# Half of a projection's weights by another queue, two convolutions moved between engines, and a new order of work

## The chip, the core and the metric

The program runs on one NeuronCore of a Trainium2 chip. The core has four compute engines with an instruction queue each, which they work through in order: TensorE (PE; its weight loads are listed as PEld), VectorE (DVE), ScalarE (ACT) and GpSimd (POOL). SyncE (SP) computes nothing here; it issues DMAs. Sixteen DMA engines move data between HBM and the on-chip memory SBUF. Matmuls write to PSUM, eight banks of 512 fp32 columns, and VectorE or ScalarE read the results out of it. Engines wait for one another through semaphores. The metric is the device time of one execution in microseconds; a profiled execution shows when each instruction ran.

## What is computed

Eight batches of an attention without softmax (8 heads, 576 positions, 64 per head), normed per head, followed by a gated feed-forward block with a convolution over three positions:

```
kv  = einsum('bhsd,bhse->bhde', k, v)
out = einsum('bhsd,bhde->bhse', q, kv)
out = out / sqrt(mean(out*out, -1) + 1e-6) * g_norm
x   = out, heads side by side                       # 8 x 576 x 512
h   = max(x @ w_in, 0)                              # 8 x 576 x 1024
c   = conv_w[0]*h[s-1] + conv_w[1]*h[s] + conv_w[2]*h[s+1]
y   = (h * sigmoid(c)) @ w_out                      # 8 x 576 x 512
```

All inputs and the output are fp32 in HBM; the kernel works in bf16 with fp32 sums.

## The kernel before

The kernel is a set of small operations, each a Python function of two to four letters, and a long string ORDER (lines 59 to 135) that names them one by one. The loop at line 779 issues them in that order, and lines 786 to 794 forbid any reordering within an engine. A token such as `hk.0.3.1.0@0` is the operation, its arguments, and after the @ the slots of the buffer rings or PSUM banks that it takes. So ORDER fixes, for each engine on its own, the sequence of work; where an operand isn't ready, the engine stands with all that is behind it. The arguments are mostly b (batch), u (half of the head pairs), s (half of the positions), f (one of 8 blocks of 128 channels of d_ff), j (a pair of such blocks), and for the output p (pair of batches) and m (one of 9 blocks of 128 rows).

What the operations do, by engine:

- Loads. `pre` (247) issues batch 0 in fp32, by the plain queues of SyncE and ScalarE as the table HEAD says (233): q and k by SyncE, v by ScalarE. `cad` and `caa` (389, 392) cast these to bf16 on VectorE and ScalarE. All later batches come by GpSimd's queue, whose DMAs cast on the way: `Lq`, `Lk`, `Lv` (350 to 356); so do `Li` (359, w_in) and `Lo` (364, w_out). `gt` (375) is a tiny GpSimd copy that waits for one of the fp32 tiles and so holds back what GpSimd issues behind it.
- TensorE. `fi` (283) multiplies zeros by zeros, n times 512 columns; it is filler that keeps the array running. `ct` transposes the convolution weights. `qt` (425) transposes q, `kv` (395) makes k-transposed v, `ot` (454) the attention's output, `on` and `oq` (524, 531) sum its squares over each head with a matrix of ones, in whole or in quarters of the array. `hk` (652) is two of the four matmuls of x @ w_in for one f and one half s; `hs` and `hm` are the same for later batches. `cv` (701) is the convolution of one f by six matmuls with an identity and two diagonal matrices, which `dg` (310) prepares on VectorE. `om` (727) is half of y's sum for a row block, `oh` (753) a last row block by column halves.
- VectorE and ScalarE. `qa`/`qd` and `kva`/`kvd` copy q transposed and kv from PSUM (a on ScalarE, d on VectorE). `sq`, `nl` (506, 541): squares and reciprocal square roots on ScalarE; `mo` (555) multiplies the norm in and writes x on VectorE. `rp`, `rh`, `re`: the relu on ScalarE. The convolution of a pair j without TensorE is `ta` for each f, `aa` and `ab` (678 to 692) on VectorE, then `sg` (695) on ScalarE, the sigmoid; with TensorE it is `cv` and `sc` (713, the sigmoid out of PSUM). `mg` (720) multiplies by h. `nl` and the sigmoids need different function tables, and ScalarE loads a table at each change (227).
- Output. `ea` on ScalarE or `ed` on VectorE copy a row block to a slot of the ring "row", `st` stores it by SyncE; `eh`/`dh` and `sh` do it for a column half.

`pl`, `ps`, `pn`, `pg` and `pc` are VectorE's preparations of constants (selection matrices, convolution weights).

In the old order batch 0's blocks 0 to 3 (j = 0 and 1) are convolved on TensorE (`cv.0.2 cv.0.3 cv.0.1 cv.0.0`), all others on VectorE. The first half of w_in is `Li.0.4`, the first cast load that GpSimd issues, after `gt.k.1.0`.

## Time and profile before

| | |
|---|---|
| time, median of 3 runs | 177.79 us (177.78 to 178.52) |
| profiled execution, its span | 175.6 us |
| TensorE busy | 96% of the span |
| VectorE and ScalarE busy | 85% each |
| GpSimd busy | 13% |
| read from HBM, written | 32.52 MB, 9.44 MB |
| cast loads (q0), their packets' time | 14.50 MB, 49.2% of 16 engines' span |
| plain queues (q1) | 13.11 MB, 26.2% |

A row of the profile has a line of the kernel, an engine, an operation, the names out<-in, the tile's partitions x elements with its type, and a count. In the view in order of time the first two numbers are start and duration in us, and a bracket tells how long the engine stood idle before it and what released it. In the view by groups the numbers behind the bar are total busy us and mean ns of one. In the view of stretches each row has from:to, length, then busy us and count for PE, PEld, DVE, ACT and POOL, then the granted share of the TensorE clock, the DMA engines' load and GB/s. The page's rows of digits cut the span in 40 slices of 4.39 us; each digit is the busy tenth. Matmuls overlap in their pipeline, so their single durations are longer than the steps from one to the next.

### The profile page before, as it was taken

What the parts mean: (1) busy time and instruction counts of PE and PEld (TensorE: products, weight loads), DVE (VectorE), ACT (ScalarE), POOL (GpSimd) and SP (SyncE); (2) the same over time, 40 slices, a digit from 0 to 9 for tenths busy, and PEclk for the clock granted to TensorE, in tenths of its full rate; (3) what the DMA queues carried; (4) which work ended last, traced back from release to release, by engine and by line L of the source; (5) the groups of instructions that cost most, each with busy time, mean ns of one, the idle gap of its engine ahead of it and who ended that gap; (6) DMA issues with size and microseconds to landing.
All of it is one profiled execution on the core that took longest, in us unless ns stands there. A gap on an engine that the chain in (4) does not pass through costs nothing.

```text
span 175.6 us, 5070 instructions
## 1 busy us (share of the span) xinstructions
PE 167.9 (96%) x2097; PEld 100.0 (57%) x2114; DVE 149.5 (85%) x290; ACT 148.9 (85%) x268; POOL 22.2 (13%) x35
## 2 busy tenths in 40 slices
PE   7979999999999999999999999999999999999992
...
GB/s 159 392 323 207 207 207 207 208 208 209 207 241 230 227 207 207 170 182 197 258 181 161 14 134 0 119 123 0 119 63 0 0 0 116 13 239 175 179 304 237
DMA packets 25911, 29.11 MB, mean 166 GB/s; under 512 B 6036, under 2 KB 20384, under 8 KB 25888
## 3 DMA queue, kind: packets, MB, share of 16 engines
q0 software_dynamic: 13296, 14.50, 49.2%
q1 hardware_dynamic: 12048, 13.11, 26.2%
q10 hardware_dynamic: 544, 1.18, 1.7%
...
HBM read 32.52 MB, written 9.44 MB: 239 GB/s over the span
## 4 chain that ended last, share of the span: by engine, by line
PE 76%; DVE 12%; ACT 5%; DMA 3%; issue 3%; ACTq 0%; DVEq 0%
PE banks L732 32%; PE banks L628 14%; PE banks L613 9%; PE banks L658 4%; DMA stg<-in_v_dram 3%; PE banks L460 3%; DVE h L722 2%; PE banks L708 2%; ACT taps L698 2%; PE banks L402 2%; PE banks L593 2%; PE banks L433 1%; PE banks L528 1%; DVE taps L681 1%; PE banks L286 1%
## 5 line engine op out<-in xcount | busy, mean ns | idle before, releaser
L732 PE MATMUL banks<-w_out_sb,h 128*128 128x512 bf16 x267 | 62.8, 379 | 1.2 <-issue 0.6
L698 ACT ACTIVATE taps<-taps,cw 128x576 bf16<-128x576 bf16 (+1 forms) x44 | 40.6, 958 | 5.7 <-DVE taps L692 5.5
L732 PEld LDWEIGHTS <-h 128*128 128x128 bf16 x280 | 26.2, 98 | 30.0 <-issue 1.1
L628 PE MATMUL banks<-x,w_in_sb 128*128 128x288 bf16 (+2 forms) x256 | 34.2, 286 | 0.0
L640 ACT ACTIVATE h<-banks 128x288 bf16<-128x288 f32 (+2 forms) x80 | 29.5, 460 | 0.3 <-PE banks L658 0.2
L628 PEld LDWEIGHTS <-w_in_sb 128*128 128x128 bf16 x256 | 24.4, 98 | 7.8 <-issue 0.8
L722 DVE TENSOR_TENSOR h<-h,taps 128x1152 bf16<-128x1152 bf16 (+1 forms) x24 | 22.8, 952 | 1.2 <-ACT taps L698 1.2
L687 DVE TENSOR_TENSOR taps<-taps 128x1152 bf16<-128x1152 bf16 (+1 forms) x22 | 21.5, 978 | 0.5
L509 ACT ACTIVATE sq<-banks 128x576 bf16<-128x576 f32 (+2 forms) x32 | 20.8, 691 | 1.1 <-PE banks L460 1.1
L692 DVE TENSOR_TENSOR taps<-taps,h 128x1152 bf16<-128x1152 bf16 (+1 forms) x22 | 21.4, 972 | 0.3
L681 DVE TENSOR_SCALAR taps<-h,cw 128x576 bf16<-128x576 bf16 (+1 forms) x44 | 18.7, 424 | 0.6 <-ACT h L665 0.5
L682 DVE TENSOR_SCALAR taps<-h,cw 128x576 bf16<-128x576 bf16 (+1 forms) x44 | 18.4, 418 | 0.0
L738 ACT ACTIVATE row<-banks 128x512 f32<-128x512 f32 x23 | 13.5, 597 | 5.7 <-PE banks L732 4.2
L658 PE MATMUL banks<-x,w_in_sb 128*128 128x288 bf16 (+2 forms) x128 | 17.7, 286 | 0.1
L613 PE MATMUL banks<-x,w_in_sb 128*128 128x288 bf16 x128 | 16.9, 286 | 0.0
L556 DVE SCALAR_TENSOR_TENSOR x<-banks,cw,rs 128x576 bf16<-128x576 f32 (+2 forms) x16 | 13.0, 816 | 3.9 <-ACT rs L545 3.6
L658 PEld LDWEIGHTS <-w_in_sb 128*128 128x128 bf16 x128 | 12.0, 98 | 4.4 <-issue 0.5
L227 ACT ACT_TABLE_LOAD x10 | 12.8, 1283 | 2.0 <-issue 1.8
L613 PEld LDWEIGHTS <-w_in_sb 128*128 128x128 bf16 x128 | 12.3, 98 | 3.7 <-issue 0.2
L443 DVE COPY qT<-banks 128x1152 bf16<-128x1152 bf16 (+2 forms) x13 | 8.8, 681 | 5.7 <-PE banks L433 5.7
L545 ACT ACTIVATE rs<-banks,eps_sb 128x576 f32<-128x576 f32 (+2 forms) x16 | 11.8, 740 | 1.1 <-PE banks L528 1.1
L599 DVE SCALAR_TENSOR_TENSOR x<-o,cw,banks 128x576 bf16<-128x576 f32 (+2 forms) x16 | 12.1, 810 | 0.7 <-PE banks L593 0.5
...
## 6 DMA issues: line engine op xcount, KB each, us to landing
...
q_sb<-in_q_dram POOLq DMA_DIRECT2D x6, 576.0 KB, 17.9
k_sb<-in_k_dram POOLq DMA_DIRECT2D x6, 576.0 KB, 14.5
v_sb<-in_v_dram POOLq DMA_DIRECT2D x6, 576.0 KB, 17.9
...
```

What stands on the lines that cost most here:

```text
L509: nc.scalar.activation(T["sq", b, u, s], T["o", b, u, s], AX.Square)
L613: nc.tensor.matmul(ps[:, s, :HS], w_in_sb[:, t, f * P:(f + 1) * P], T["x", b][:, t, c0:c1], start=(t == 0), stop=(t == NT - 1))
L628: nc.tensor.matmul(ps, w_in_sb[:, t, f * P:(f + 1) * P], T["x", b][:, t, c0:c1], start=(t == 0), stop=(t == NT - 1))
L640: nc.scalar.activation(h, fr, AX.Relu)
L658: nc.tensor.matmul(T[at], w_in_sb[:, t, f * P:(f + 1) * P], T["x", b][:, t, c0:c1], start=(t == 0), stop=(t == NT - 1))
L681: nc.vector.tensor_scalar_mul(tap[:, 0, f % 2, :n, 8:8 + S], h[:, f], cw[:, f:f + 1])
L682: nc.vector.tensor_scalar_mul(tap[:, 1, f % 2, :n, :S], h[:, f], cw[:, 2 * NF + f:2 * NF + f + 1])
L687: nc.vector.tensor_add(tap[:, 1, :, :n, :S], tap[:, 0, :, :n, 7:7 + S], tap[:, 1, :, :n, 1:1 + S])
L692: nc.vector.tensor_add(y, y, span(b, n)[:, 2 * j:2 * j + 2])
L698: nc.scalar.activation(y, y, AX.Sigmoid, scale=cw[:, NF + f:NF + f + 1])
L722: nc.vector.tensor_mul(h, h, tap_of(b, j)[:, 1, :, :n, :S])
L732: nc.tensor.matmul(T["om", p, m], h[:, f, m * P:(m + 1) * P], w_out_sb[:, f, :], start=(f == 0), stop=(f == NF - 1))
```

## The change

Batch 0's loads by SyncE are put in another sequence (k's tiles 2 and 3 ahead of the second q), and behind them SyncE loads the first half of w_in in fp32, in two pieces of 256 columns (512 KB each), into two slots of the ring "x". `wd` casts a piece to bf16 on VectorE (`wa`, on ScalarE, isn't used). `Li.0.4` is gone; GpSimd's loads begin after `gt.q.1.1` and come in another sequence. Batch 0's pair j = 1 (blocks 2 and 3) is convolved on VectorE (`ta`, `aa`, `ab`, `sg`) instead of TensorE, and two `dg` are gone. Two of batch 0's casts, one copy of q and two of kv go from VectorE to ScalarE; two `on` become `oq`. The 12 groups of fillers (37 matmuls) become 7 groups (39): 20 ahead of the first transposes, 8 and 4 ahead of the first kv, 7 more up to the first `hk`, none behind it. The order of the whole string is new on every engine, and so are its slots; the output's evictions are shared out differently, several stores are issued later, and both halves of the last row block use slot 5. The number of sigmoid and norm table changes stays 10.

```diff
-    HEAD = (("sync", "q.0.0 k.0.1 k.1.1 q.1.0 k.2.1 k.3.1 q.0.1 q.1.1"), ("scalar", "v.0.2 v.2.2"))
+    HEAD = (("sync", "q.0.0 k.0.1 k.1.1 k.2.1 k.3.1 q.1.0 q.0.1 q.1.1 w.0.2 w.2.2"), ("scalar", "v.0.2 v.2.2"))
...
+    w_rows = moe_w_in.rearrange("(t p) f -> p t f", p=P)
...
-                if x == "q":
+                if x == "w":
+                    T["stw", t] = ring("x", [P, NT, s * P], FP32, "stw")
+                    queue.dma_start(out=T["stw", t], in_=w_rows[:, :, t * P:(t + s) * P])
+                elif x == "q":
...
+    @op
+    def wd(f0, n):
+        nc.vector.tensor_copy(w_in_sb[:, :, f0 * P:(f0 + n) * P], T["stw", f0])
...
-        if u0 == 0:
+        if ("kvb", b) not in T:
...
-        if s == 0:
+        if ("qT", b, u) not in T:
```

The beginning of ORDER:

```diff
-pre@0,1 af cad.q.0.0@0 cad.v.0.0@0 fi.10.512@0 qt.0.0.0@2 qd.0.0.0@0 gt.k.1.0 Li.0.4 fi.9.512@0 ct@0 Lq.1.0.2@1
-Lk.1.0.2@0 Lv.1.0.2@1 Li.4.4 ps pg fi.4.512@1 cad.k.1.0@1 caa.v.1.0 caa.k.0.0 kv.0.0.1@4 kva.0.0.1@0 ot.0.0.0@6 pc
...
-sq.0.1.1@3 oq.0.0.1@0 nl.0.0.1@2 fi.1.512@4 fi.1.512@4 hk.0.1.0.0@4 hk.0.1.0.1 rp.1.0@0 on.0.1.1@0 nl.0.1.1@3
...
-hk.0.2.1.1 qt.1.0.0@6 kv.1.0.1@4 rp.2.1 cv.0.2@2 sc.0.2@0 cv.0.3@0 qd.1.0.0@2 kvd.1.0.1@1 ot.1.0.1@6 sc.0.3 pl
+pre@0,1,0,1 af pl ps caa.q.0.0@0 caa.v.0.0@0 fi.20.512@0 qt.0.0.0@0 qa.0.0.0@0 pn caa.k.0.0@1 cad.v.1.0 fi.8.512@2
+ct@0 pg caa.k.1.0 pc caa.v.2.0 fi.4.512@1 kv.0.0.1@0 kva.0.0.1@0 cad.k.2.0 fi.2.512@2 ot.0.0.0@0 cad.v.3.0 sq.0.0.0@0
+cad.k.3.0 fi.3.512@2 oq.0.0.0@2 cad.q.1.0 kv.0.1.1@4 nl.0.0.0@0 dg.0 qt.0.1.0@6 kva.0.1.1 qd.0.1.0@1 caa.q.0.1
+mo.0.0.0@2 ot.0.1.0@2 sq.0.1.0@0 gt.q.1.1 fi.1.512@4 qt.0.0.1@4 cad.q.1.1 Lv.1.0.2@1 qa.0.0.1 oq.0.1.0@0 dg.1
+qt.0.1.1@6 Li.4.4 nl.0.1.0@0 ot.0.0.1@4 qd.0.1.1 sq.0.0.1@0 wd.0.2 ot.0.1.1@0 Lq.1.0.2@1 sq.0.1.1@1 mo.0.1.0
+fi.1.512@6 oq.0.0.1@6 Lk.1.0.2@0 nl.0.0.1@1 wd.2.2 oq.0.1.1@2 Lq.1.2.2 nl.0.1.1@0 hk.0.0.0.0@6 mo.0.0.1 hk.0.0.0.1
+Lk.1.2.2 hk.0.3.0.0@7 hk.0.3.0.1 mo.0.1.1 hk.0.2.0.0@2 Lv.1.2.2 rp.3.0@0 hk.0.2.0.1 hk.0.1.1.0@3 rp.0.0 hk.0.2.1.0@4
+rp.2.0 Lk.2.0.4@1 hk.0.2.1.1 hk.0.3.1.0@5 rp.2.1 hk.0.3.1.1 Lq.2.0.4@0 hk.0.1.1.1 ta.0.1.2@1 rp.3.1 hk.0.1.0.0@2
+hk.0.1.0.1 rp.1.1 hk.0.0.1.0@4 ta.0.1.3 Lo.0.8 rp.1.0 hk.0.0.1.1 hk.0.5.1.0@5 aa.0.1.1 cv.0.1@0 ab.0.1.1 Lv.2.0.4@0
+qt.1.0.0@2 sc.0.1@0 hk.0.5.0.0@6 qd.1.0.0@0 hk.0.5.1.1 rp.0.1 hk.0.5.0.1 sg.0.1.3 kv.1.0.1@0 Lq.3.0.4@2 cv.0.0@2
+kvd.1.0.1@0 sg.0.1.2 hk.0.7.0.0@4 rp.5.0 mg.0.1.1 qt.1.1.0@0 sc.0.0 ot.1.0.1@6 hk.0.7.0.1 qd.1.1.0@1 sq.1.0.1@0
+hk.0.4.1.0@2 hk.0.7.1.0@3 mg.0.1.0 hk.0.4.1.1 hk.0.7.1.1 oq.1.0.1@0 nl.1.0.1@0 rp.5.1 ot.1.0.0@0 mo.1.0.1@0 rp.7.0
+sq.1.0.0@0 kv.1.1.1@4 ta.0.1.5@0 rp.7.1 Lv.3.0.4@1 on.1.0.0@6 kvd.1.1.1 rp.4.1 ta.0.1.7@1 hk.0.4.0.0@3 nl.1.0.0@0
...
```

Its end:

```diff
-ed.3.7@4 om.3.5.4.4 ea.3.5@3 st.3.5 om.3.4.4.4 ed.3.4@5 st.3.4 st.3.7 om.3.6.4.4 ea.3.6@0 st.3.6 oh.3.8.1@1 eh.3.8.1@2
-sh.3.8.1 oh.3.8.0@0 eh.3.8.0@1 sh.3.8.0
+om.3.5.4.4 ed.3.7@0 om.3.4.4.4 ed.3.5@2 oh.3.8.1@0 st.3.5 ea.3.4@4 om.3.6.0.4@1 dh.3.8.1@5 sh.3.8.1 om.3.6.4.4 st.3.7
+st.3.2 oh.3.8.0@0 st.2.3 ea.3.6@2 st.3.4 st.3.6 eh.3.8.0@5 sh.3.8.0
```

134 lines of the change are left out of this document (64 added, 70 removed).

## The prediction

> **What bounds the kernel now.** I read the page first, then the busy times of four stretches, then TensorE and ScalarE in order of time at the start, then the groups of instructions for prices.
>
> ```profile
> span 175.6 us, 5070 instructions
> PE 167.9 (96%) x2097; PEld 100.0 (57%) x2114; DVE 149.5 (85%) x290; ACT 148.9 (85%) x268; POOL 22.2 (13%) x35
> ...
> PE   7979999999999999999999999999999999999992
> ...
> GB/s 159 392 323 207 207 207 207 208 208 209 207 241 230 227 207 207 170 182 197 258 181 161 14 134 0 119 123 0 119 63 0 0 0 116 13 239 175 179 304 237
> ```
> ```profile
> 0.00:21.20 21.20, 18.64 (x238) 9.22 (x241) 13.91 (x54) 12.27 (x23) 10.69 (x20) 1.00 1.02 260
> 21.20:30.60 9.40, 9.20 (x212) 6.21 (x213) 5.13 (x19) 9.34 (x17) 2.14 (x4) 1.00 1.22 206
> 30.60:172.20 141.60, 140.09 (x1651) 84.57 (x1662) 130.45 (x218) 126.87 (x229) 9.34 (x13) 1.00 0.72 148
> 172.20:175.60 3.40, 0.00 (x0) 0.00 (x0) 0.00 (x0) 0.38 (x1) 0.00 (x0) 1.00 0.54 194
> ```
>
> TensorE is the bound: from 30.6 to 172.2 us it idles 141.60 - 140.09 = 1.51 us in all, and then 3.4 us remain for the last eviction and store. In the first 21.2 us it idles 2.6 us, and part of its busy time there is fillers. From 21.2 to 30.6 ScalarE is as full (9.34 of 9.40) while VectorE has 4.3 us free. So one question decides: by how much is TensorE earlier or later than today when it reaches the work that both kernels have in common after about 30 us? What it is late there, it can win back only out of those 1.51 us.
>
> ```profile
> 1.20 4.45 PE L286 MATMUL banks<-zero 128*128 128x512 bf16 x10 [1.20 <-DVE zero L265]
> 5.57 0.32 PE L433 MATMUL banks<-ident,q_sb 64*64 64x64 bf16 x16
> 5.83 2.12 PE L286 MATMUL banks<-zero 128*128 128x512 bf16 x9
> 7.87 0.24 PE L291 MATMUL banks<-ident,cw_rows 25*128 25x25 f32 x1
> 8.04 1.04 PE L286 MATMUL banks<-zero 128*128 128x512 bf16 x4
> 9.57 0.47 PE L402 MATMUL banks<-v_sb,k_sb 64*64 64x64 bf16 x34 [0.34 <-DVE k_sb L384]
> 13.25 0.30 PE L460 MATMUL banks<-qT,kvb 64*64 64x256 bf16 x4
> 17.64 3.65 PE L658 MATMUL banks<-x,w_in_sb 128*128 128x256 bf16 x28
> 21.22 0.48 PE L433 MATMUL banks<-ident,q_sb 64*64 64x64 bf16 x36
> 30.59 1.15 PE L658 MATMUL banks<-x,w_in_sb 128*128 128x256 bf16 x8
> ```
> ```profile
> 10.10 0.28 ACT L416 ACTIVATE kvb<-banks 128x128 bf16<-128x128 f32 x1 [2.55 <-PE banks L402]
> 14.70 0.69 ACT L545 ACTIVATE rs<-banks,eps_sb 128x512 f32<-128x512 f32 x1
> 21.82 1.28 ACT L227 ACT_TABLE_LOAD   x1
> 27.60 0.74 ACT L545 ACTIVATE rs<-banks,eps_sb 128x576 f32<-128x576 f32 x1
> 16.87 0.91 POOL L365 DMA_DIRECT2D w_out_sb<-in_moe_w_out_dram  x1 [2.30 <-DMA w_in_sb<-in_moe_w_in_dram]
> ```
>
> Columns are start, duration, engine, line, operation, count. The first ten fillers take 0.43 us each (4.45 for ten), the nine at 5.83 only 0.21 (2.12, less 0.2 of latency): TensorE is slow until about 5.5 us. The POOL row shows that the first half of w_in lands at about 16.8, just before the 28 matmuls of 17.64.
>
> **The change, part by part: the first 23 us.** Prices of groups, the last number the mean in ns:
>
> ```profile
> L384 DVE CAST v_sb<-stg 128x576 bf16<-128x576 f32 x2 | 0.9, 457 | 0.2 <-DMA stg<-in_v_dram 0.2
> ...
> L384 DVE CAST q_sb<-stq 128x512 bf16<-128x512 f32 x1 | 0.4, 427 | 1.9 <-DMA stq<-in_q_dram 1.9
> ...
> L386 ACT ACTIVATE v_sb<-stg 128x576 bf16<-128x576 f32 x2 | 1.4, 680 | 2.5 <-DMA stg<-in_v_dram 2.5
> ...
> L443 DVE COPY qT<-banks 128x512 bf16<-128x512 bf16 x2 | 0.8, 414 | 0.0
> ...
> L556 DVE SCALAR_TENSOR_TENSOR x<-banks,cw,rs 128x512 bf16<-128x512 f32 x2 | 1.5, 741 | 0.0
> L556 DVE SCALAR_TENSOR_TENSOR x<-banks,cw,rs 128x640 bf16<-128x640 f32 x2 | 1.8, 884 | 0.9 <-ACT rs L545 0.9
> ...
> L509 ACT ACTIVATE sq<-banks 128x640 bf16<-128x640 f32 x6 | 4.2, 721 | 0.0
> ...
> L665 ACT ACTIVATE h<-banks 128x256 bf16<-128x256 f32 x8 | 3.5, 455 | 0.4 <-PE banks L658 0.4
> ```
>
> Ahead of the first k-v product the old order has 10 + 9 + 4 = 23 fillers, the new one 20 + 8 + 4 = 32, and TensorE keeps the order. Twenty from 1.20: ten at 0.43 to 5.5, ten at 0.21 to 7.6. Then qt.0.0.0 to 7.9 (before 5.57), eight fillers to 9.6, ct, four more to 10.6; kv.0.0.1 stands at 10.7 to 11.2 instead of 9.57 to 10.04. K tile 1 isn't the limit any more: ScalarE casts it after qa.0.0.0 (7.98 to 8.6) and k tile 0, 0.65 us each, by 9.9. So kva.0.0.1 starts at 11.25 (before 10.10).
>
> [...]
>
> ScalarE then goes sq, nl.0.0.0 (13.0 to 13.7), kva.0.1.1 to 14.0. TensorE's ot.0.1.0 stands at 14.1 (before 13.25). Ahead of its square ScalarE now has caa.q.0.1 (0.70), and ahead of nl.0.1.0 the copy qa.0.0.1 (0.65): nl.0.1.0 moves from 14.70 to 15.95. VectorE: four casts moved behind pg and pc end at 13.1; qd.0.1.0 to 14.1, mo.0.0.0 (0.74), cad.q.1.1, dg.1, qd.0.1.1 (0.41, after its transposes) to 16.5.
>
> Then the two new casts of w_in, 1024 elements each. No row has that size: the slope from 512 to 576 (30 ns for 64) gives 0.67 us, proportion to the 457 ns gives 0.81, and twice that, under load from other traffic, 1.6; I take 0.67 as nearest to the rows' own slope. Arrival: at the 392 GB/s of the second slice the three tensors of 1.18 MB are there by about 11.6 and 1.05 MB of w_in by about 14.5, with competition perhaps 16.5, so the landing hides behind the chain. wd.0.2 runs 16.5 to 17.15, mo.0.1.0 to 17.9, wd.2.2 to 18.55, mo.0.0.1 (0.88) to 19.4, mo.0.1.1 to 20.3. What is queued behind the two casts are the three mo of batch 0, and TensorE waits for them. hk.0.3.0.0 needs wd.2.2 and the bank that nl.0.0.1 frees at 18.7; its 28 matmuls at today's 3.65 us end at 22.45. Before, TensorE was through at 21.22: **+1.25 us**.
>
> **From there to 31 us.** Removed on TensorE: two convolutions of six matmuls (one pair in the chain of waits is 1.59 us) and the three fillers that the old order has after this point (0.64). That alone would more than repay the 1.25. But the convolutions' place is taken by two ordinary sets of taps:
>
> ```profile
> 22.05 1.59 PE banks L708 x12
> ```
> ```profile
> L681 DVE TENSOR_SCALAR taps<-h,cw 128x576 bf16<-128x576 bf16 x28 | 10.4, 373 | 0.6 <-ACT h L665 0.5
> L682 DVE TENSOR_SCALAR taps<-h,cw 128x576 bf16<-128x576 bf16 x28 | 10.2, 364 | 0.0
> ...
> L687 DVE TENSOR_TENSOR taps<-taps 128x1152 bf16<-128x1152 bf16 x14 | 10.6, 759 | 0.3
> ...
> L698 ACT ACTIVATE taps<-taps,cw 128x576 bf16<-128x576 bf16 x28 | 20.7, 777 | 5.6 <-DVE taps L692 5.5
> L715 ACT ACTIVATE taps<-banks,cw 128x576 bf16<-128x576 f32 x4 | 2.8, 746 | 0.0
> ```
>
> VectorE gets 2 x (0.37 + 0.36) + 2 x 0.76 = 3.0 us more, which its 4.3 free us cover; two sigmoids from taps for two from PSUM leave ScalarE the same (0.78 for 0.75). ScalarE is the stage's limit, however. Its last rp ahead of the sigmoid table (rp.1.0; the six matmuls behind hk.0.1.0.1 don't concern it) now ends at 22.5, and the table load goes there from 21.82. From it to nl.1.0.1 the new order has: load 1.28, sc 0.7, rp.0.1 0.42, two sg 1.5, rp.5.0 0.42, sc 0.7, sq 0.65, load 1.28 = 6.95 us, against 27.60 - 21.82 = 5.78. So nl.1.0.1 starts at 29.4 instead of 27.60. And TensorE waits for it: oq.1.0.1 and the next ot.1.0.0 are both written at banks 0 and 1, so ot.1.0.0 stands until nl.1.0.1 has read them (30.1), with everything behind it. Then rp.5.1, rp.7.0, sq.1.0.0, rp.7.1 free the bank of hk.0.4.0.0 at about 32.05. In the old kernel those matmuls stand at 30.59, with ot.1.1.1 (0.3) already done: TensorE is **1.75 us late** with the removed 2.2 us of work already counted. Bounds: 0.5 (clock up early, casts 0.67, ScalarE's pieces at their back-to-back spacing) to 3.0 (late clock, casts 1.6).
>
> **After 31 us** the matmuls are the same ones, so the lateness passes through. The idle 1.51 us can shrink to nothing (-1.5) or grow (+2: VectorE gets evictions 1.0, 1.1 and 1.8 that ScalarE had); I take 0. The later start of the cast loads costs nothing: those 0.5 MB of w_in no longer stand ahead of them.
>
> **The tail.**
>
> ```profile
> 172.27 0.38 ACT L767 ACTIVATE row<-banks 128x256 f32<-128x256 f32 x1 [0.54 <-PE banks L757]
> ```
> ```profile
> L777 SPq DMA_DIRECT2D out_dram<-row x2: 333/350/368, 171.8 to 172.7; - x2
> ...
> DMA to landing us min/median/max: 1.9/2.2/2.5
> ```
>
> Both halves of the last row now use row slot 5, so eh.3.8.0 must wait until sh.3.8.1 has landed: from the end of oh.3.8.1 0.4 (eviction) + 0.35 (issue) + 2.2 = 2.95 us, against 2.6 us of matmuls meanwhile (om.3.6 and oh.3.8.0: eight of 512 columns at the 0.21 of the fillers, eight of 256 at half): +0.3 (0 to +0.8, as five full stores queue between the halves).
>
> **Sum**, against the profiled execution: 1.75 + 0 + 0.3 = +2.05 us on a span of 175.6. The median run is 177.79, 2.19 more than that span; the same surplus gives 177.79 + 2.05 = 179.8.
>
> **Rivals.** *TensorE's own work decides* (faster): nl.1.0.1 comes before TensorE needs banks 0 and 1, so nothing holds it between 22 and 30 us. Then the start costs 1.25, the removed 1.59 + 0.64 count in full, and with a third of the later idle gone it is -1.48, 176.3. It decides if nl.1.0.1 starts before 28.3. For it: TensorE is 96% busy; against it: ScalarE's 9.34 of 9.40 and the shared banks. *The lateness is eaten*: 1.75 late at 31, but nearly all of the 1.51 of idle vanishes: 178.2. For it: VectorE and ScalarE have 11.2 and 14.7 us free after 30.6; against it: most of that is behind 140 us or in other places than TensorE's. *ScalarE and VectorE stay behind*: the backlog starves TensorE again in the later stages, +3 more, 182.8; against it, three evictions leave ScalarE.
>
> **How the numbers follow.** The forecast 0.57 (its own range 178.7 to 181.4), TensorE's work 0.15, eaten 0.13, behind 0.15. About 0.9 us either side of 177.79 can't be told from no change: faster 0.15, same 0.13, slower 0.72. The range 176.5 to 182.6 leaves out about half of the first and the last rival.
>
> **What would show it.** Right: k-v product of batch 0 after 10.5 us; qt.1.0.0 after 22; TensorE idle over 1 us before ot.1.0.0, released by ScalarE's L545; the last eviction released by a store. Wrong: the first product still at 9.6, no TensorE idle from 23 to 32 us, or a later idle under 0.8 us.

## The result, and the profile after

The changed kernel takes 188.92 us (median of 4 runs, 186.48 to 190.62) against 177.81 us for the kernel before on the same chip: a ratio of 1.0575, 95% interval 1.0507 to 1.0643. The forecast was 179.8 us with a range to 182.6, so the sign was right and the size was wrong by 9 us. Executions more than 1.5% above the fastest of their kernel (one of the changed kernel's, one each of e2_row and e12_wpool, two of e9_all, one of them its traced one) are left out of the ratios; by its ratio the changed kernel stands at 188.0 us. The profiled execution spans 187.0 us, 11.4 more than the 175.6 of before.

The page of the changed kernel: span, busy time, TensorE's slices and the granted clock.

```profile
span 187.0 us, 5079 instructions
PE 171.6 (92%) x2108; PEld 100.7 (54%) x2108; DVE 150.8 (81%) x290; ACT 152.6 (82%) x272; POOL 21.4 (11%) x34
...
PE   7988997999899979999579999999999999999980
...
PEclk9999998799999999999988999999999999999998
```

TensorE lost four points of its share. The slices, 4.7 us each, show where: at the 7th and 8th TensorE has a dent and the clock another; at the 11th and 15th TensorE alone; at the 20th to 22nd TensorE and then the clock; and the last slice is empty. From the 23rd to the 38th all is full. So the loss isn't one long wait; it sits in a few places, and TensorE's rows in order of time name them. The changed kernel:

```profile
10.37 0.48 PE L415 MATMUL banks<-v_sb,k_sb 64*64 64x64 bf16 x36
17.99 4.35 PE L671 MATMUL banks<-x,w_in_sb 128*128 128x256 bf16 x34 [0.18 <-ACT rs L558]
29.32 0.32 PE L473 MATMUL banks<-qT,kvb 64*64 64x288 bf16 x4 [0.99 <-ACT rs L558]
30.01 0.48 PE L415 MATMUL banks<-v_sb,k_sb 64*64 64x64 bf16 x36 [0.38 <-ACT h L678]
30.86 0.38 PE L671 MATMUL banks<-x,w_in_sb 128*128 128x256 bf16 x2
44.42 0.78 PE L415 MATMUL banks<-v_sb,k_sb 64*64 64x64 bf16 x72
48.62 0.38 PE L446 MATMUL banks<-ident,q_sb 64*64 64x64 bf16 x23 [0.92 <-issue]
69.70 0.71 PE L415 MATMUL banks<-v_sb,k_sb 64*64 64x64 bf16 x64 [1.16 <-issue]
91.00 0.78 PE L492 MATMUL banks<-v_sb,k_sb 64*64 64x64 bf16 x72 [2.38 <-DMA k_sb<-in_k_dram]
96.13 0.70 PE L606 MATMUL banks<-wparts,spread 32*128 32x288 bf16 x4 [1.24 <-ACT h L653]
105.88 0.79 PE L492 MATMUL banks<-v_sb,k_sb 64*64 64x64 bf16 x72
```

The kernel before, the three products that can be matched with it:

```profile
43.17 0.78 PE L402 MATMUL banks<-v_sb,k_sb 64*64 64x64 bf16 x72
...
84.28 0.78 PE L479 MATMUL banks<-v_sb,k_sb 64*64 64x64 bf16 x72
...
96.55 0.79 PE L479 MATMUL banks<-v_sb,k_sb 64*64 64x64 bf16 x72
```

Stretches of the changed kernel, cut where the granted clock changes (the column behind the five engines is the granted clock, PEclk):

```profile
28.25:31.65 3.40, 2.03 (x52) 1.22 (x50) 2.35 (x6) 3.39 (x9) 0.84 (x2) 1.00 1.21 208
31.66:35.06 3.40, 3.40 (x18) 1.68 (x16) 2.19 (x5) 2.52 (x6) 1.37 (x2) 0.50 1.23 206
...
93.10:96.50 3.40, 2.09 (x20) 1.25 (x17) 2.13 (x3) 1.32 (x4) 0.00 (x0) 1.00 0.58 165
96.52:99.92 3.40, 3.40 (x17) 1.51 (x17) 2.14 (x3) 3.21 (x5) 0.00 (x0) 0.50 1.30 198
```

Matching points of equal work gives the lateness step by step. Where the two orders have not done the same work at a point, the difference is added (the kernel before has `ot.1.1.1`, 0.25 us, done ahead of `hk.0.4.0.0`, and `om.0.2.0.4`, four matmuls of 0.21 us, ahead of `kv.2.0.2`). Of the 34 matmuls in the row at 17.99 the last two are `hk.0.5.1.0`, which the kernel before does later, so the first line of the table counts 32.

| TensorE reaches | before | after | late by | what came in |
|---|---|---|---|---|
| end of batch 0's first 32 `hk` matmuls | 21.2 | 21.9 | 0.7 | the start |
| `hk.0.4.0.0` | 30.6 | 30.9 (+0.25) | 0.5 | two convolutions and three fillers gone, waits of 0.99 and 0.38 |
| `kv.2.0.2` | 43.2 | 44.4 (+0.86) | 2.1 | half clock for 3.4 us: 1.6 |
| `kz.6.0.2` | 84.3 | 91.0 | 6.7 | two stops of 0.92 and 1.16, and 2.38 for batch 6's k |
| `kz.7.0.2` | 96.5 | 105.9 | 9.3 | 1.24 for ScalarE, and half clock: 1.4 |
| last matmul's end | 172.2 | 181.5 | 9.3 | nothing: the last 76 us cost the same |
| end | 175.6 | 187.0 | 11.4 | tail 5.5 instead of 3.4 |

Three of these have their cause in rows of other engines. GpSimd issues a k only when its slot is free. The last two k of the changed kernel, and in a second fence the last two of the kernel before:

```profile
70.74 0.74 POOL L352 DMA_DIRECT2D k_sb<-in_k_dram  x1 [13.20 <-PE banks L415]
...
80.38 0.74 POOL L352 DMA_DIRECT2D k_sb<-in_k_dram  x1 [7.42 <-PE banks L473]
```
```profile
67.96 0.74 POOL L347 DMA_DIRECT2D k_sb<-in_k_dram  x1 [2.52 <-PE banks L402]
...
75.01 0.74 POOL L347 DMA_DIRECT2D k_sb<-in_k_dram  x1 [5.57 <-PE banks L460]
```

Before, the first of each two is batch 6 and the second batch 7. In the new order the first is batch 7 and the second batch 6, which is needed 15 us sooner: its load is issued at 80.38 instead of 67.96, and it lands some 10.6 us later, when `kz.6.0.2` has waited 2.38 us for it.

ScalarE's eviction `ea.0.6` waits for a slot of the ring "row" whose store hasn't landed, and the row of SyncE's queue says why (the line's own view gives 2.0 us as the shortest, 2.4 as the median and 11.6 as the longest time from issue to landing):

```profile
95.18 0.60 ACT L751 ACTIVATE row<-banks 128x512 f32<-128x512 f32 x1 [3.33 <-DMA out_dram<-row]
```
```profile
80.82 2.55 SPq L480 DMA_TRANSPOSE qT<-q_sb  x1
83.47 3.60 SPq L761 DMA_DIRECT2D out_dram<-row  x2
```
```profile
DMA to landing us min/median/max: 2.0/2.4/11.6
```

The store stands right behind a DMA transpose and needs 11.6 us. But the DMA engines are full here (a load of 1.0 to 1.4 in stretches of 5 us from 60 to 95 us), and other stores of this stage are slow too, without a transpose right ahead of all of them: those issued at 67.5 to 86.7 us took 5.3 to 8.9 us, and the kernel before has 6.6 to 7.8 us for three of its own at 80 to 85 us. How much of the 11.6 us is the transpose's own isn't shown by any run. TensorE's 1.24 us before L606 are the end of this: `rh` stands behind `ea.0.6` on ScalarE. And the tail:

```profile
179.41 0.33 SPq L790 DMA_DIRECT2D out_dram<-row  x1
179.80 2.75 SPq L761 DMA_DIRECT2D out_dram<-row  x5
...
181.56 0.38 ACT L780 ACTIVATE row<-banks 128x256 f32<-128x256 f32 x1 [0.28 <-PE banks L770]
182.65 0.40 SPq L790 DMA_DIRECT2D out_dram<-row  x1
```

The last eviction is released by TensorE, not by a store, and is done at 181.9. Its store is issued 0.7 us later, because five full stores that the old order spread out are ahead of it, and it lands 4.3 us after its issue.

### The profile page after: what moved, and what is told of

Its sections match the earlier page's. It is cut to its first block, busy times and chain, and to the rows that moved or that the text cites. A ratio compares the mean times of both kernels' runs of the same rounds, so it can differ in the third digit from the quotient of the medians.

```text
span 187.0 us, 5079 instructions
## 1 busy us (share of the span) xinstructions
PE 171.6 (92%) x2108; PEld 100.7 (54%) x2108; DVE 150.8 (81%) x290; ACT 152.6 (82%) x272; POOL 21.4 (11%) x34
## 3 DMA queue, kind: packets, MB, share of 16 engines
q10 hardware_dynamic: 544, 1.18, 1.6%
## 4 chain that ended last, share of the span: by engine, by line
PE 75%; DVE 7%; DMA 6%; ACT 6%; issue 3%; ACTq 0%
PE banks L745 26%; PE banks L641 13%; PE banks L671 10%; PE banks L626 9%; DMA out_dram<-row 6%; PE banks L291 5%; PE banks L446 2%; PE banks L415 2%; PE banks L473 1%; ACT rs L558 1%; DVE taps L695 1%; PE banks L550 1%; PE banks L541 1%; DVE taps L700 1%; DVE h L735 1%
## 5 line engine op out<-in xcount | busy, mean ns | idle before, releaser
L745 PE MATMUL banks<-w_out_sb,h 128*128 128x512 bf16 x280 | 64.3, 379 | 0.0
L711 ACT ACTIVATE taps<-taps,cw 128x576 bf16<-128x576 bf16 (+1 forms) x46 | 41.4, 951 | 2.5 <-DVE taps L705 2.4
L641 PE MATMUL banks<-x,w_in_sb 128*128 128x288 bf16 (+2 forms) x256 | 34.3, 286 | 0.0
L641 PEld LDWEIGHTS <-w_in_sb 128*128 128x128 bf16 x256 | 24.3, 98 | 8.0 <-issue 0.9
L522 ACT ACTIVATE sq<-banks 128x576 bf16<-128x576 f32 (+2 forms) x32 | 21.1, 694 | 2.2 <-PE banks L473 1.6
L700 DVE TENSOR_TENSOR taps<-taps 128x1152 bf16<-128x1152 bf16 (+1 forms) x23 | 22.1, 966 | 0.4
L705 DVE TENSOR_TENSOR taps<-taps,h 128x1152 bf16<-128x1152 bf16 (+1 forms) x23 | 22.1, 962 | 0.2
L694 DVE TENSOR_SCALAR taps<-h,cw 128x576 bf16<-128x576 bf16 (+1 forms) x46 | 19.3, 420 | 1.7 <-ACT h L678 1.3
L695 DVE TENSOR_SCALAR taps<-h,cw 128x576 bf16<-128x576 bf16 (+1 forms) x46 | 19.7, 429 | 0.0
L671 PE MATMUL banks<-x,w_in_sb 128*128 128x288 bf16 (+2 forms) x128 | 19.3, 300 | 0.2 <-ACT rs L558 0.2
L626 PE MATMUL banks<-x,w_in_sb 128*128 128x288 bf16 x128 | 17.9, 298 | 0.0
L671 PEld LDWEIGHTS <-w_in_sb 128*128 128x128 bf16 x128 | 12.4, 102 | 5.2 <-issue 0.8
L626 PEld LDWEIGHTS <-w_in_sb 128*128 128x128 bf16 x128 | 12.7, 101 | 4.7 <-issue 0.7
L558 ACT ACTIVATE rs<-banks,eps_sb 128x576 f32<-128x576 f32 (+2 forms) x16 | 11.8, 743 | 2.9 <-PE banks L541 1.5
L291 PE MATMUL banks<-zero 128*128 128x512 bf16 x39 | 11.2, 428 | 1.2 <-DVE zero L270 1.2
```

The source lines that it names most:

```text
L291: nc.tensor.matmul(ps[:, :w], zero[:, :P], zero[:, :w], start=True, stop=True)
L522: nc.scalar.activation(T["sq", b, u, s], T["o", b, u, s], AX.Square)
L626: nc.tensor.matmul(ps[:, s, :HS], w_in_sb[:, t, f * P:(f + 1) * P], T["x", b][:, t, c0:c1], start=(t == 0), stop=(t == NT - 1))
L641: nc.tensor.matmul(ps, w_in_sb[:, t, f * P:(f + 1) * P], T["x", b][:, t, c0:c1], start=(t == 0), stop=(t == NT - 1))
L671: nc.tensor.matmul(T[at], w_in_sb[:, t, f * P:(f + 1) * P], T["x", b][:, t, c0:c1], start=(t == 0), stop=(t == NT - 1))
L695: nc.vector.tensor_scalar_mul(tap[:, 1, f % 2, :n, :S], h[:, f], cw[:, 2 * NF + f:2 * NF + f + 1])
```

## The experiments

All stand against runs of the kernel before on the same chip (177.6 or 177.7 us each time). Times below are the ratio times 177.6; the changed kernel is 187.8 on this scale, ratio 1.058 (1.051 to 1.064).

| run | base and edit | us | ratio, 95% interval |
|---|---|---|---|
| e1_k6 | after; k slots of batches 6 and 7 exchanged | 189.6 | 1.068 (1.062 to 1.073) |
| e2_row | after; `ea.0.6` on row slot 3 | 185.2 | 1.043 (1.036 to 1.050) |
| e3_k6_row | both | 183.5 | 1.033 (1.031 to 1.035) |
| e4_fill | after; 16 fillers in the gaps at 28 to 30 us | 186.3 | 1.049 (1.046 to 1.052) |
| e5_shift | after; 16 tiny fillers early, no gap filled | 187.9 | 1.058 (1.052 to 1.064) |
| e6_wsync | before; first half of w_in by SyncE | 184.7 | 1.040 (1.036 to 1.044) |
| e7_cvd | before; two convolutions on VectorE | 179.5 | 1.011 (1.010 to 1.013) |
| e8_tail | e3; late stores behind their evictions | 181.4 | 1.021 (1.018 to 1.025) |
| e9_all | e8; 16 fillers in the gaps | 180.2 | 1.015 (1.013 to 1.017) |
| e10_open | e9; ten of the opening fillers 32 wide | 178.5 | 1.005 (1.004 to 1.006) |
| e11_vec | e8; two evictions on VectorE, `kv.1.1.1` moved | 179.8 | 1.013 (1.011 to 1.014) |
| e12_wpool | e9; w_in by GpSimd again | 179.6 | 1.011 (1.009 to 1.013) |
| e13_open_wpool | e10 and e12 together | 178.9 | 1.008 (1.006 to 1.009) |
| e14_vec | e8; two evictions on VectorE | 179.8 | 1.012 (1.011 to 1.014) |
| e15_best | e8; e10, e12 and e14 together | 179.8 | 1.013 (1.010 to 1.015) |
| e16_open_vec | e8; e10 and e14 together | 179.3 | 1.010 (1.007 to 1.012) |
| e17_pool1 | e13; GpSimd's loads in another sequence, 24 fillers | 179.4 | 1.010 (1.008 to 1.012) |
| e18_pool2 | e17; GpSimd's loads released earlier | 177.7 | 1.000 (0.999 to 1.002) |

**The waits at 91 and 96 us.** Three runs: the k slots exchanged, the row slot changed, and both.

```diff
-Lk.7.0.4@1
+Lk.6.0.4@1
...
-Lk.6.0.4@0
+Lk.7.0.4@0
...
-ea.0.6@2
+ea.0.6@3
```

> The changed kernel, but batch 6's k takes the slot that batch 4's k leaves, and batch 7's k the one that batch 5's leaves (it is the other way round in the change). Theory A, two stops in series: TensorE's wait of 2.9 us for batch 6's k (88 to 91 us) goes, but ScalarE still stands until a store has landed at about 95 us and stops TensorE there, so less than 1.5 us is gained. Rival B, the late k alone makes this stage slow: 2.9 us and the half-rate stretch behind it (1.4) are gained, 4 us or more.

> The changed kernel, but the eviction ea.0.6 takes row slot 3 instead of 2, whose store lands 11.6 us after its issue. Theory A (two stops in series): ScalarE's 3.3 us wait for that landing goes, TensorE's stop at 95 us (1.2 us) goes, the wait for batch 6's k stays: 1 to 2.7 us gained, the latter if the half-rate stretch from 96.8 us goes too. Rival B (the late k alone): 0.5 us or less.

> Both edits of the two kernels before together. Theory A: TensorE's idle of 3.7 us between 88 and 96 us goes and, since the array then never idles there, the half-rate stretch behind it (1.4 us) too: 4.5 to 6 us gained, more than the sum of the two alone. Rival B: as with the k alone, about 4 us. Rival C, the half-rate stretches have nothing to do with the stops: 3.7 us, and the granted clock still falls near 97 us.

The first gained nothing (if anything it lost 1%), the second gained 1.4% and both together 2.3%. TensorE's rows of the three show the two waits as stops in series: with the k there in time, TensorE comes to L606 earlier and waits longer for ScalarE, 2.81 us instead of 1.24. First e1_k6, then e2_row, then e3_k6_row:

```profile
95.19 0.60 PE L606 MATMUL banks<-wparts,spread 32*128 32x288 bf16 x4 [2.81 <-ACT h L653]
```
```profile
88.39 0.78 PE L492 MATMUL banks<-v_sb,k_sb 64*64 64x64 bf16 x72 [1.21 <-DMA k_sb<-in_k_dram]
```
```profile
92.12 0.60 PE L606 MATMUL banks<-wparts,spread 32*128 32x288 bf16 x4 [0.24 <-ACT h L653]
```

In the last one TensorE's clock is at 1.00 through these stages. So the two waits and the clock that they cost are worth 4.3 us (187.8 to 183.5), just under the least that theory A said. Rival B had some 4 us for the late k alone; e1_k6, which gained nothing, rules it out. The last row's wait of 0.24 is what is left of both.

**The stops marked "issue".** In the changed kernel TensorE stops for 0.92 and 1.16 us in the middle of one operation, with all operands there. Counted along the order, the two places are behind its 733rd and its 1116th matmul. The difference is 383, three times 128 but one; with a weight load for each (the page has 2108 of both), 128 matmuls are 256 instructions. The page lists 16 packets on the queue "instruction" with 0.26 MB, 16 KB each; TensorE has 2 x 2108 instructions, 264 for each packet, and one such packet moves in the 2 us around each stop's beginning (46 to 48 and 67 to 69 us). From these numbers I estimated that the stops are borders between two blocks of instructions. No run shows what a stop waits for; "border" below means the place in the count. e4_fill puts 16 matmuls into the gaps at 28 to 30 us, e5_shift the same number, 32 columns wide, at 13.8 us, where they fill nothing.

```diff
-ot.0.1.0@2 sq.0.1.0@0
+ot.0.1.0@2 fj.16.0.32@4 sq.0.1.0@0
...
+    def fj(n, c0, w):
+        ps = bank()
+        for _ in range(n):
+            nc.tensor.matmul(ps[:, c0:c0 + w], zero[:, :P], zero[:, :w], start=True, stop=True)
```

> The changed kernel with 12 and 4 short fillers (192 columns, 0.08 us each) in the two gaps of TensorE around 28.3 to 30 us, written to unused columns of a bank. They fill the idle time and remove no wait. Theory A: the clock then stays at full rate from 31 to 35 us, where it was halved for 3.8 us, and 1.9 us are gained (1.4 to 2.2). Rival C (the clock falls for another reason): nothing gained, or 0.3 lost, and the granted clock at 32 to 36 us stays near 0.6.

> The changed kernel with 16 matmuls of 128x32 on zeros more at about 13.8 us, ahead of all else: some 0.5 us of extra work, no idle time filled. Theory F (the stops of 0.92 and 1.16 us in the middle of L446 and L415 hang on how many instructions TensorE has run before them): both stops leave their places, since every later TensorE instruction now stands 32 places (weight load and matmul) further on; if they find no other burst of short instructions, the time falls by 1 to 2 us from the changed kernel's 188.9, and if they only move to another line it stays within 1 us. Rival T (they hang on the time, on other traffic or on an operand): they stay after 49 and after 8 of their instructions, and the time is the same or 0.5 us longer.

In e5_shift both stops left their places; TensorE's row there:

```profile
69.07 0.25 PE L452 MATMUL banks<-ident,q_sb 64*64 64x64 bf16 x7 [0.29 <-issue]
```

Seven of `qt.4.1.0`'s 36 transposes are left, so this border is behind matmul 1117, within one of the number before, now in another operation. e4_fill stops at the same number for 0.29 us, and for 0.84 us behind matmul 1244, some 128 later. e7_cvd, built on the kernel before with 12 matmuls fewer, has a new stop of 1.00 us inside `kv.4.0.2`, behind matmul 1116. The number decides, not the operation, its operand or the time: theory F holds for the place. For the length, the starts of the matmuls in the traces say how fast the 128 ahead of a border went by, from the first start to the last: 3.0 and 2.8 us at the two stops of the changed kernel; about 4.5 us in e4_fill and e5_shift where they don't stop, and 4.6 where they stop for 0.29; 4.7 us and more in the kernel before, which shows no stop. That looks as if only a fast 128 were followed by a long stop. But in e7_cvd the 128 took 3.9 us ahead of a stop of 1.00, and at e4_fill's stop of 0.84 they took 6 us or more. So theory F holds for the place, and what makes a stop long or short stays open. The time of e5_shift is another matter: 187.9 us is no change, where F expected 1 to 2 us less. Its profiled execution gained 1.8 us on the stops and had a half-clock stretch from 18.8 us, as long as the changed kernel's at 31.7, and `ot.1.0.0` at 32.2 instead of 29.3. The time of e4_fill is 1.6 us better, as theory A said, and its trace has no half-clock stretch at 31 us any more, only one from 89.5 us. But the time mixes the filled gaps and the clock with the moved borders and a wait for batch 6's k that grew to 3.15 us, and prices none of them alone.

**The tail.** e8_tail has e3's two mends, and each late store right behind its own eviction:

```diff
-ed.3.7@0 om.3.4.4.4 ed.3.5@2 oh.3.8.1@0 st.3.5 ea.3.4@4 om.3.6.0.4@1 dh.3.8.1@5 sh.3.8.1 om.3.6.4.4 st.3.7
-st.3.2 oh.3.8.0@0 st.2.3 ea.3.6@2 st.3.4 st.3.6 eh.3.8.0@5 sh.3.8.0
+ed.3.7@0 st.3.7 om.3.4.4.4 ed.3.5@2 oh.3.8.1@0 st.3.5 ea.3.4@4 st.3.4 om.3.6.0.4@1 dh.3.8.1@5
+sh.3.8.1 om.3.6.4.4 oh.3.8.0@0 ea.3.6@2 st.3.6 eh.3.8.0@1 sh.3.8.0
```

> The changed kernel with the k slots of batches 6 and 7 exchanged and ea.0.6 on row slot 3 (as in the run of both, 183.6 us), and now also each late store issued right behind its own eviction and the last half row on a slot of its own. Theory P (the five full stores in front of the last one, 2.75 us at 179.8 us, and the shared slot make the tail 5.5 instead of 3.4 us): the tail falls to 3.4 to 3.9 us and the time to 181.5 to 182.2 us. Rival V (the tail is set by how much is still to be moved at the end): it stays above 4.8 us and the time within 0.5 us of 183.6.

```profile
175.22 0.33 SPq L761 DMA_DIRECT2D out_dram<-row  x1
175.52 0.38 ACT L780 ACTIVATE row<-banks 128x256 f32<-128x256 f32 x1 [0.33 <-PE banks L770]
175.93 0.33 SPq L790 DMA_DIRECT2D out_dram<-row  x1
```

The last store is issued when its eviction is done, 175.9, and the kernel ends at 179.0, 3.6 us after the last matmul: 2.1 us gained, theory P.

**The load of w_in, alone.** e6_wsync is the kernel before with SyncE's fp32 load (`w.0.2 w.2.2` at the end of its head) and two casts on VectorE, nothing else but the place of one `dg`:

```diff
-pre@0,1 af cad.q.0.0@0 cad.v.0.0@0 fi.10.512@0 qt.0.0.0@2 qd.0.0.0@0 gt.k.1.0 Li.0.4 fi.9.512@0
+pre@0,1,1,2 af cad.q.0.0@0 cad.v.0.0@0 fi.10.512@0 qt.0.0.0@2 qd.0.0.0@0 gt.k.1.0 fi.9.512@0
...
-qd.0.1.1 mo.0.1.0 ot.0.0.1@2
+qd.0.1.1 mo.0.1.0 wd.0.2 wd.2.2 ot.0.0.1@2
```

> The kernel before with only the first half of w_in by SyncE's queue in fp32 and two casts of it on VectorE after mo.0.1.0 (0.7 us each in the changed kernel's trace): nothing else moved but the two halves of its issue and one diagonal. Theory S (the load and its casts are the dear part of the start): the three mo of batch 0 and with them hk come 1.0 to 1.5 us later, +0.8 to +1.5 us against the kernel before, 178.4 to 179.2. Rival N (the casts hide behind ScalarE's squares and nl): within 0.5 us of the kernel before. Rival G (POOL's load was the wait ahead of hk): 0.5 to 1 us faster.

It cost 7.1 us, far outside all three. VectorE's casts and TensorE behind them, in e6_wsync:

```profile
16.97 0.69 DVE L370 CAST w_in_sb<-stw 128x1024 bf16<-128x1024 f32 x1 [0.89 <-DMA stw<-in_moe_w_in_dram]
21.13 0.69 DVE L370 CAST w_in_sb<-stw 128x1024 bf16<-128x1024 f32 x1 [3.46 <-DMA stw<-in_moe_w_in_dram]
```
```profile
21.88 2.53 PE L671 MATMUL banks<-x,w_in_sb 128*128 128x256 bf16 x11 [3.28 <-DVE w_in_sb L370]
```

The second piece lands at 21.1 us; in the changed kernel, where its cast starts at 17.5, it waits only 0.2 us. What differs is GpSimd's queue. In e6_wsync it issues its first load at 8.4 us, as before, and eight loads, w_out's 1 MB among them, by 14.8; the DMA engines are full (a load of 1.1 to 1.2 from 8.4 to 21.1 us) and SyncE's fp32 pieces share them. In the changed kernel `gt.q.1.1` holds the first of these loads until 13.2, and w_out's is issued at 21.5. This fits the late landing, but no run has e6's load with the later release, so it isn't shown by itself that the later release is what pays for the fp32 load. As it stands, e6's is the worst single edit of this study. TensorE's pause also cost clock: the stretch from 20.2 to 27.0 us has a PEclk of 0.50.

**Two convolutions on VectorE, alone.** e7_cvd moves blocks 2 and 3 of batch 0 to VectorE in the kernel before (the first line of the cut gathers tokens from several places of the order):

```diff
-dg.3 dg.2 cv.0.2@2 sc.0.2@0 cv.0.3@0 sc.0.3
...
-kvd.1.0.1@1 ot.1.0.1@6
+kvd.1.0.1@1 ta.0.1.2@0 ta.0.1.3 aa.0.1.1 ab.0.1.1 cv.0.1@4 cv.0.0@2 sc.0.1@1 sc.0.0 ot.1.0.1@6
...
-mg.0.1.1 Lo.0.8
+sg.0.1.2 sg.0.1.3 Lo.0.8 mg.0.1.1
```

> The kernel before with only two of batch 0's convolutions (blocks 2 and 3) moved from TensorE to VectorE. Theory S (ScalarE bounds 22 to 31 us): TensorE's 1.6 us of work goes, but nl.1.0.1 comes at the same time, so TensorE waits for it in their place: within 0.5 us of the kernel before. Rival W (TensorE's own work decides): 1.0 to 1.6 us faster. Rival L (VectorE's 3 us more delay qd.1.1.0 and batch 1): 0.5 to 2 us slower.

It is 2.0 us slower. TensorE's rows:

```profile
22.71 0.41 PE L708 MATMUL banks<-h,ident 128*128 128x288 bf16 x2 [0.72 <-DVE kvb L414]
...
29.11 0.48 PE L402 MATMUL banks<-v_sb,k_sb 64*64 64x64 bf16 x36 [0.66 <-ACT rs L545]
...
69.36 0.50 PE L402 MATMUL banks<-v_sb,k_sb 64*64 64x64 bf16 x38 [1.00 <-issue]
```

The first of these waits is for VectorE's copy of kv, which is no later than before. Its row in e7_cvd, then in the kernel before:

```profile
22.38 0.28 DVE L414 CAST kvb<-banks 128x128 bf16<-128x128 f32 x1
```
```profile
22.43 0.28 DVE L414 CAST kvb<-banks 128x128 bf16<-128x128 f32 x1
```

What changed is that `cv.0.1` takes bank 4 of `kv.1.0.1` right behind it, where the old order had the two convolutions in between. The second wait, for ScalarE's nl, hangs on the first: the late `cv.0.1` makes `sc.0.1` late, ScalarE stands 0.61 us for it, and nl.1.0.1 starts at 28.31 instead of 27.60. So these two come of the order that this edit chose, and neither rival L (VectorE's added work) nor theory S is shown by them. The third is the border described above, which 12 fewer matmuls moved there. TensorE's busy time fell by 0.9 us (167.9 to 167.0) and its idle time grew by 3.0, of which the three waits are 2.4. The run doesn't price the removal of the convolutions alone.

**The opening fillers, and w_in again.** e9_all puts the 16 fillers of e4 on top of e8. In e10_open ten of the opening twenty are 32 columns wide, which leaves the number of instructions as it is; e12_wpool gives the first half of w_in back to GpSimd; e13_open_wpool has both.

```diff
-fi.20.512@0 qt.0.0.0@0
+fi.10.512@0 fi.10.32@0 qt.0.0.0@0
```

e12's edit, which e13 has too (`w.0.2 w.2.2` goes from SyncE's head, both `wd` go):

```diff
-pre@0,1,0,1
+pre@0,1
...
-kva.0.0.1@0 cad.k.2.0
+kva.0.0.1@0 gt.k.1.0 Li.0.4 cad.k.2.0
```

> The changed kernel with exchanged k slots, ea.0.6 on slot 3, the late stores behind their own evictions (the run at 181.4 us) and 16 matmuls of 128x192 on zeros at 28 to 30 us, where TensorE waits 1.0 and 0.4 us for ScalarE. Theory F (a stop stands where 256 TensorE instructions, loads and matmuls, go by in less than about 4 us, and the 16 pairs move the border out of the burst): the stops of 0.87 and 1.16 us go, one of 0.3 us appears in qt.4.1.0, 179.6 to 179.9 us. Rival T (the stops hang on time or traffic): they stay, and 181.4 us stays. Rival C (the clock falls when TensorE idles, and this is what the fillers mend): no more to gain, since the profile at 181.4 us shows no halved stretch.

> As the run with all mends and the 16 fillers, but ten of the opening twenty matmuls on zeros are 32 columns wide instead of 512: the number of TensorE's instructions stays, 2 to 4 us of opening work goes. Theory O (the opening fillers are what makes batch 0's products late): qt.0.0.0 comes at 5.6 instead of 7.2 to 8 us, the first product of k and v about 0.5 to 1 us earlier, and the time falls by 0.5 to 1.0 us. Rival N (ScalarE's chain of casts and squares sets the start, and fillers only fill): qt.0.0.0 moves, hk.0.0.0.0 does not, within 0.3 us. Rival K (fewer fillers delay the clock): half rate until 8 us or longer, 0 to 1.5 us slower.

> As the run with all mends and the 16 fillers, but the first half of w_in comes by POOL's queue in bf16 as in the kernel before (issued when k tile 1 of batch 0 is there), and VectorE has no cast of it. Theory S (the two casts of 0.7 us hold the mo of batch 0): hk.0.0.0.0 starts 0.7 to 1.4 us earlier and the time falls by 0.5 to 1.2 us. Rival N (ScalarE's nl and sq hold the mo anyway): within 0.3 us. Rival D (POOL's load slows the fp32 loads of q and v): the start is later by 0.5 us or more.

> Ten narrow opening fillers and the first half of w_in by POOL's queue together, on top of all mends and the 16 fillers at 28 to 30 us. Theory S (with the narrow fillers w_in's landing at 15.9 us and its casts hold VectorE, and TensorE waits 1.5 us for them): without the casts this wait goes and 177.3 to 178.0 us. Rival P (POOL's bf16 half lands no earlier than 16.5 us): the wait stays at hk.0.0.0.0, 178.3 to 178.8 us. Rival D (its load delays batch 0's fp32 loads): 179 us or more.

The 16 pairs brought 181.4 to 180.2 us, where F had 179.6 to 179.9. That the two long stops are gone is seen in e10_open and e12_wpool, which keep the pairs: these stop for 0.39 and 0.36 us at matmul 1117, and e12_wpool for 0.29 at 1244. The 1.2 us also holds the gaps that the pairs fill; the two parts aren't separated. F's 256 instructions in under 4 us were an estimate from the counts and the 3.0, 2.8 and 4.5 us above; e4_fill's stop of 0.84 us, behind 6 us or more, doesn't fit it. The narrow fillers gave 1.7 us more, above theory O's 1.0, and brought the kernel to 0.5% above the one before; with GpSimd's load of w_in the same edit is worth only 0.6 to 0.7 us (e12_wpool to e13_open_wpool). What the fillers delay is one step further on than expected: `ct` stands behind them on TensorE, VectorE's `pg` waits for `ct`, and four casts of k, v and q stand behind `pg`. VectorE's row for that step, in e12_wpool with wide fillers, then in e10_open:

```profile
10.63 0.18 DVE L306 COPY cw<-banks 128x25 f32<-128x25 f32 x1 [2.99 <-PE banks L302]
```
```profile
7.93 0.18 DVE L306 COPY cw<-banks 128x25 f32<-128x25 f32 x1 [0.28 <-PE banks L302]
```

The clock has a part in this difference: it rose at 6.6 us in the first of the two executions and at 3.8 us in the second.

With the start early, the load of w_in became the next limit: in e10_open VectorE waits 1.29 us for the first piece until 15.9 and TensorE 1.50 us for the x behind it. With wide fillers GpSimd's load is 0.7 us better than SyncE's with its casts, in the middle of what theory S gave; with narrow fillers it is 0.5 us worse. There the wait of 1.50 is gone, as S said, but TensorE then waits 0.80 us for w_in's second half at 21.5 us. The time, 178.9 us (178.7 to 179.2), lies between rival P's range and rival D's, and the cause is neither's.

**ScalarE's stretch from 20 to 33 us.** e11_vec and e14_vec give two of its evictions to VectorE. In e11_vec `kv.1.1.1` is also written over a bank that still holds part of `ot.1.0.1`, so part of batch 1 isn't the reference's. The cut below is e14's; in e11_vec `vp.5.1` stands ahead of `oq.1.0.1`, `vp.7.0` ahead of `nl.1.0.1`, and `kv.1.1.1` takes bank 5.

```diff
+    def vp(f, s):
+        r0, r1 = RS[s]
+        nc.vector.tensor_scalar_max(
+            h_of(0, f).rearrange("p (e n r) -> p e n r", e=2, r=R)[:, :, :, r0:r1],
+            T["hp", f, s].rearrange("p (e r n) -> p e n r", e=2, r=r1 - r0), 0.0)
...
-mg.0.1.1
+vp.5.1 mg.0.1.1
-mg.0.1.0
+vp.7.0 mg.0.1.0
-nl.1.0.1@0 rp.5.1 ot.1.0.0@0 mo.1.0.1@0 rp.7.0 sq.1.0.0@0 kv.1.1.1@4
+nl.1.0.1@0 fj.16.320.32@3 kv.1.1.1@4 ot.1.0.0@0 mo.1.0.1@0 sq.1.0.0@0
```

> As the run at 181.4 us, but the evictions rp.5.1 and rp.7.0 go to VectorE (a maximum with zero) ahead of mo.1.0.1, where it idles 1.4 us, kv.1.1.1 goes ahead of ot.1.0.0 into the bank that this frees, and 16 matmuls of 128x32 on zeros stand in what is left of the gap. Theory S (full ScalarE and taken banks cost TensorE the 1.4 us at 28 to 30 us, and the stops go with the 16 more pairs): TensorE's waits there fall to 0.3 us or less and 178.3 to 179.0 us. Rival V (VectorE is late with mo.1.0.1 by these two, 0.8 us each, and ot.1.1.1 waits in its place): 179.4 to 180.2 us.

> As the run at 181.4 us, but rp.5.1 and rp.7.0 are evicted by VectorE (a maximum with zero), the first ahead of mg.0.1.1 and the second ahead of mg.0.1.0, kv.1.1.1 stands ahead of ot.1.0.0 in its old banks, and 16 matmuls of 128x32 on zeros stand before it. Theory S (full ScalarE and taken banks cost the 1.4 us at 28 to 30 us): TensorE's waits there fall under 0.6 us, kv.1.1.1 runs before ot.1.0.0, and with the two stops gone 178.6 to 179.4 us. Rival V (VectorE is late by these two): 179.8 us or more.

Both came to 179.8 us, no better than the 180.2 that fillers alone give by more than the intervals allow. In e14_vec the waits of 0.98 and 0.37 are gone and a new one stands 1.1 us later:

```profile
31.45 0.40 PE L547 MATMUL banks<-sq,ones 128*128 128x288 bf16 x2 [0.81 <-DVE taps L707]
```

The row names VectorE, but `on.1.0.0` needs `sq.1.0.0` of ScalarE, which runs from 30.75 to 31.40. ScalarE itself stood 0.47 us for `ot.1.0.0`, which starts at 30.33, when `nl.1.0.1` (29.54, 0.74 us) is done. So the wait moved by one operation along the chain nl.1.0.1, ot, sq, on. The two evictions that VectorE took had stood behind `nl.1.0.1` on ScalarE, so this edit couldn't bring it forward; ahead of it ScalarE has no pause from 23.05 us on. That ScalarE's sum of work up to `nl.1.0.1` decides the stretch fits this, but isn't shown by it.

**All together.** e15_best and e16_open_vec join the mends, e17_pool1 and e18_pool2 leave VectorE's evictions out and take away the waits for loads that e13 still shows. e17 to e13:

```diff
-gt.q.1.1 fi.1.512@4 qt.0.0.1@4 cad.q.1.1 Lv.1.0.2@1
+gt.q.1.1 fi.1.512@4 qt.0.0.1@4 cad.q.1.1 Li.4.4 Lq.1.0.2@1 Lv.1.0.2@1
```

and in e18_pool2 `gt.q.1.0` stands in place of `gt.q.1.1`.

> All of it: exchanged k slots, slot 3 for ea.0.6, stores behind their evictions, narrow opening fillers, w_in by POOL's queue, two evictions on VectorE. If the terms add up (from 181.4 us: stops -1.2, opening -1.7, w_in -0.5, banks -0.8): 176.8 to 177.4 us, as fast as the kernel before or 0.4% faster. Rival H (ScalarE's 12 us without a pause from 20 us on hides part of the opening's gain): 177.8 to 178.4 us.

> As the last one, with the change's own load of w_in (SyncE's queue in fp32 and two casts on VectorE). Theory S (the casts cost about 0.5 to 1 us once the opening is short): 177.7 to 178.3 us. Rival N (the casts cost nothing): the same as the run with POOL's load, within 0.3 us.

> As the run with narrow opening fillers and POOL's load of w_in, but the second half of w_in and batch 1's first q go ahead of its v on POOL's queue, and 24 matmuls on zeros instead of 16 stand at 28 to 30 us, so that no 256 TensorE instructions go by in under 4 us. Theory S (the landing of w_in's second half at 21.4 us and the stops of 0.2 to 0.3 us are what is left): the waits of 0.80 and 0.24 us go and 177.4 to 178.0 us, no slower than the kernel before. Rival H (ScalarE's full stretch from 20 us takes the gain): 178.5 to 178.9 us.

> As the one before, with POOL's loads released by the third q tile instead of the last (some 2 us earlier). Theory S: the second half of w_in lands 1 to 2 us earlier, 177.2 to 177.8 us. Rival D (they take bandwidth from batch 0's last q and delay the start): 0.3 to 1 us slower than the one before.

The sum that e15_best was to show doesn't hold: 179.8 instead of 176.8 to 177.4. Its trace has a wait of 1.36 us for batch 1's q at 23.6 us and one of 1.12 us at 74.4, put down to ScalarE but behind matmul 1244. e16 with SyncE's load is no slower than e15. e17_pool1 lost 1.18 us to batch 1's k and 1.32 us in a stop at 73.1 us, behind matmul 1244. That is a border again, and the 128 matmuls ahead of it took 6.1 us, so speed doesn't explain this one either; e18_pool2, with the same TensorE order, shows 0.50 us there, put down to ScalarE. e18_pool2 is level with the kernel before (177.7 us, 0.9985 to 1.002). Its stretches and, in a second fence, TensorE's rows at 27 to 29 us:

```profile
0.00:22.34 22.34, 19.66 (x293) 10.95 (x294) 15.24 (x67) 15.88 (x28) 10.60 (x21) 1.00 1.02 255
22.34:33.45 11.11, 11.01 (x206) 7.13 (x204) 8.31 (x17) 10.91 (x21) 3.56 (x5) 1.00 1.22 207
33.45:172.30 138.85, 137.72 (x1640) 82.59 (x1637) 126.18 (x206) 124.78 (x224) 8.25 (x11) 1.00 0.72 149
```
```profile
27.11 1.16 PE L297 MATMUL banks<-zero 128*128 128x112 bf16 x20
...
28.45 0.51 PE L297 MATMUL banks<-zero 128*128 128x192 bf16 x4
```

From their first starts to the next work the two groups of fillers take 1.09 and 0.44 us, together about the 1.59 us that the two convolutions had cost, while ScalarE is busy 10.91 of 11.11 us. No kernel of this study is faster than the kernel before by a margin that the runs can show.

## Why the prediction was right and where it was wrong

**The start: right.** The forecast had the first 32 `hk` matmuls through at 22.45 us, 1.25 late; in the trace it is about 21.9, 0.7 late. The difference is the clock's: it rose at 4.35 us in this execution where the forecast took 5.5, which is luck. The k-v product was forecast at 10.7 (10.37), VectorE's casts at 0.67 us each (0.74 and 0.69), with the load hidden but for 0.20 us. It also named the longer opening as a cost; shortening it gained 1.7 us with SyncE's load of w_in (e10_open) and 0.6 to 0.7 with GpSimd's (e13_open_wpool). That "the later start of the cast loads costs nothing" was right and perhaps too weak: e6_wsync, which lacks it, is 7.1 us slower, though no run shows the later start by itself.

**From there to 31 us: right in kind, too large.** ScalarE holds TensorE at `ot.1.0.0`, as forecast: 0.99 us, then 0.38. From table load to nl.1.0.1 it took 6.5 us instead of 6.95, so nl.1.0.1 came at 28.53 and not 29.4, and TensorE was 0.5 us late at `hk.0.4.0.0` where 1.75 had been forecast, at the lower bound. The bounds of 0.5 and 3.0 rest in part on an early and a late clock, and no run shows how far these can lie apart; in the traced executions but e9_all's the clock rose between 3.8 us (e10_open) and 7.1 us (e1_k6). Nor does a run show the upper bound's cast of 1.6 us: the two took 0.74 and 0.69. e18_pool2 agrees that ScalarE's sum of work decides there (busy 10.91 of 11.11 us) and that it takes back the whole of the removed convolutions; e14_vec and e7_cvd don't settle it.

**"After 31 us the matmuls are the same ones, so the lateness passes through": this step failed.** It took 0 within -1.5 to +2; the trace has +8.8 (0.5 to 9.3). The step looked at the engines' free time in the later stages, found 11 to 15 us of it and stopped there. What came in was none of an engine's work: a load issued 12 us later because of which slot it was given (2.4 us), a ring slot whose store took 11.6 us to land (1.2), stops at borders in the count of instructions, which other counts of matmuls had moved (2.1), and half clock for 3.4 us twice, after pauses that were short by themselves (3.0). The first two are shown together by e1 to e3, whose 4.3 us hold the second half-clock stretch as well. Of the third, e4, e5 and e7 show that the place goes by the count; the price isn't shown by itself, since e5, where the stops were 1.8 us shorter, is no faster. The fourth is read off the granted clock. No run changed the clock alone, but executions of e10_open and e16_open_vec, each the same kernel, took 0.9 to 2.2 us longer at a mean clock of 0.99 than at 0.998 and more, where two stretches here are put at 1.6 and 1.4; these executions may differ in more than the clock. The first three can be seen or suspected in the change before it runs: `Lk.6` and `Lk.7` swap places in GpSimd's sequence, `ea.0.6` changes its slot, and the count of matmuls ahead of many an operation changes.

**The tail: right in sign, mis-sized, wrong in its mechanism.** +0.3 (0 to 0.8) was forecast for a last eviction that waits for the slot it shares; it costs 2.1, and that eviction waits 0.28 us, for TensorE. The cost is in the five full stores ahead of the last one, which the forecast had noted only as the reason for its upper bound.

**The rivals.** The third, +3 us in the later stages by a backlog of ScalarE and VectorE, had the right direction, but of its mechanism only the 1.24 us behind ScalarE appeared, and that was a store's. Of the signs, `qt.1.0.0` after 22 us (23.02) came true, the wait before `ot.1.0.0` was released by ScalarE as said (L558, the changed kernel's number for that line) and with 0.99 us just missed "over 1", the k-v product missed its mark of 10.5 by 0.13, and the last eviction released by a store did not come.
